# The last K and Q of batch 1: turned by DMA instead of on TensorE, with the first loads in a new order

## The chip, the cores and the metric

The kernel runs on one NeuronCore of one Trainium2 chip. The metric is the device time of one execution in microseconds (us), given as the median over runs. The engines of the core are TensorE (PE, matrix multiplication; PEld is its weight load, which overlaps), VectorE (DVE), ScalarE (ACT), GpSimd (POOL) and SyncE (SP). Here POOL does little but issue loads from HBM that cast from float32 to bf16, and SP does little but issue DMA transposes.

## The reference

Two layers, one after the other. The first is attention with a window of 32 tokens to both sides, for 8 batches of 8 heads with 576 tokens and a head size of 64. The second is a pair of dense layers (512 to 2048 to 512) with a squared ReLU between them, over all 4608 tokens.

```python
scores = scale * np.matmul(q, k.transpose(0, 1, 3, 2))
mask = np.abs(pos[:, None] - pos[None, :]) <= window
scores = np.where(mask, scores, -1000000000.0)
attn = np.exp(scores - np.max(scores, axis=-1, keepdims=True))
attn = attn / (np.sum(attn, axis=-1, keepdims=True) + 1e-09)
attn_out = np.matmul(attn, v)
x = attn_out.transpose(0, 2, 1, 3).reshape(B * S, H * D)
h = np.maximum(x @ w_in, 0.0)
out = (h * h) @ w_out
```

## The kernel before

Work is cut into 24 groups of 192 query tokens, three to a batch; group G is part g of batch b, G = 3b + g. A group has two windows, A and B, of 128 keys each. For a group the kernel does the following, and each step is an operation with a name in the program:

- It loads K, Q and V. V goes to its tile directly (`load_v`, line 443, in two pieces j = 0 and 1). The left 64 rows of V's first piece are copied from the group before (`copy_v`, line 450, on DVE).
- It turns K and Q, so that the head dimension lies on the partitions. This is done in one of two ways, below.
- It computes scores (`scores`, line 565) for all 8 heads, exponentials on ACT (line 589), the mask on DVE (line 594), and the products with V (`pv`, line 622, once for each window).
- It divides on DVE (lines 641 and 644) and turns the result into `xt`: on TensorE for the first three groups (lines 671 to 701), by two DMA transposes on SP for the others (lines 717 and 720).

The dense layers follow the tokens as they come. The up-projection (`mm1`, line 737) takes 192, later 256, later 512 tokens at a time against two slices of 128 of the 2048 hidden columns (or one slice with 512 tokens). For 192 tokens that is eight matmuls to an operation and eight operations to a block; ACT applies the ReLU (line 743), DVE squares (line 746). There are two PSUM tiles, `ht`, so an up-projection waits for the ReLU of the one before the last. The down-projection (`mm2`, line 757) takes 128 tokens and a quarter of the hidden columns at a time, four matmuls to an operation.

**K and Q, first way (groups 0 to 5).** `load_pair` loads two neighbouring tokens with one descriptor (512 bytes read, 256 written) in one DMA; a DVE copy (line 429) parts the two tokens; `turn_pe` turns the tile with eight TensorE transposes (line 485) into PSUM; ACT moves Q (line 513) and DVE moves K (line 516) to the tiles `qt` and `kt`. Group 0 alone is loaded through SP in float32 and cast on ACT and DVE (`load_hw`, lines 407 to 417).

**K and Q, second way (groups 6 to 23).** `load_qk` loads single tokens (256 bytes read, 128 written) in two DMAs, one for the first half of the tokens and one for the second; `turn_dma` turns each half with a DMA transpose that SP issues (line 524), straight into `qt` and `kt`.

**The order.** The program isn't written in the order in which it runs. Each operation is recorded with its engine, its inputs and outputs, an estimate of its duration and a key. `Prog.schedule` then plays them through: each engine takes the ready operation with the lowest key, three DMA rings (POOL, SP, ACT) share one transfer resource, and the result is a fixed order for each engine, in which `emit` writes the instructions with their semaphore waits. On the chip an engine works through its list in that order and waits where an input is late. A DMA's `slack` (`LSLACK1`, `TSLACK` and others) is a reserve added to its planned landing, so that what needs it is planned later; nothing of it is waited for on the chip.

The keys of the first loads come from the list `OPENING`, in its order: K and Q by group, V by group and piece, `w1` and `w2` the four pieces of each weight matrix, `hq` and `hk` the loads through SP. POOL issues its loads in this order, about 0.8 us apart. Loads of batch 2 and later wait for the scores of a group three before them (`gate`).

TensorE's queue is filled, while there is nothing to do at the start, with matmuls on zeros (line 322) up to the transposes of group 0's result.

`NSPLIT` says for how many groups the scores of windows A and B are recorded as two operations (eight matmuls each) instead of one (sixteen). `MKEY` and `VSET` are keys of DVE's setup of two masks and of two V tiles.

Of the kernel before, what the change touches and what calls it, by code (L numbers as in the profile page):

```python
# [20 lines left out]
NTURN = 2  # L21
NXT = 3
LEAD = 13.0
# [6 lines left out]
TDKEY = 3.0  # L30
XKEY = (0.2, 0.5)
QMOVE = 14.5
# [10 lines left out]
LSLACK = 3000  # L43
# [3 lines left out]
VCS = 6  # L47
NDUP = 1
NPR = 3
LSLACK1 = 1000  # L50
HOLD = {}
KMIN = 0.5
HOLDT = 26000
KSPL = 0
XTD = 1
NSPLIT = 3
HWB = 150
HWQ = {'k': 'SP', 'q': 'SP'}
HWC = {"k": ("DVE", "ACT"), "q": ("ACT", "DVE")}
NPAIR = 6  # L60
FIRST = {}
T512 = 2048
NBIAS = 1
PKEY = 0.2
MKEY = (-9.5, -6.5)
VSET = (-9.8, -6.8)
ESPLIT = 0
IOTA = -1
OPENING = [("k", 1), ("w1", 0), ("v", 0, 0), ("v", 1, 1), ("q", 1), ("v", 0, 1), ("q", 2), ("k", 2), ("v", 1, 0), ("w1", 1),
           ("w1", 2), ("w1", 3), ("q", 5), ("v", 2, 0), ("v", 2, 1), ("w2", 1), ("k", 3), ("v", 3, 0), ("q", 3), ("w2", 0), ("w2",  # L70
           2), ("k", 4), ("v", 3, 1), ("q", 4), ("v", 5, 0), ("v", 5, 1), ("w2", 3), ("hq", 0), ("k", 5), ("v", 4, 0), ("v", 4, 1),
           ("hk", 0)]
WARM = 40000
LAST = ((0, 256), (256, 384), (384, 512))
KC = ((0, 224), (224, 192), (416, 160))
# [204 lines left out]
class Gen:  # L280
# [105 lines left out]
    def load_qk(self, t, b, g, key):  # L386
        t0, n = KC[g] if t == "k" else (192 * g, 192)
        h = n // 2
        G = 3 * b + g
        raw = self.RAW[t][G % NRAW]  # L390
        src = (self.q if t == "q" else self.k)[b]
        s = src[:, t0:t0 + n, :].rearrange("h (j p) d -> p j h d", j=2)
        for j in range(2):
            self.p.rec("POOL", lambda e, j=j: e.dma_start(raw[0:h, j, :].rearrange("p (h d) -> p h d", h=8), s[:, j]),  # L394
                       writes=[("raw", t, G % NRAW, j)], dma=(f"{t}{G % NRAW}{j}", G), key=key, dur=500 + 3 * h,
                       move=(h // 2, QMOVE), name=f"{t}{b}{g}{j}", after=self.gate(3 * b + g), slack=LSLACK if b > 1 else 0)

    def load_hw(self, t, g, key):

# [72 lines left out]
    def turn_pe(self, t, b, g, key):  # L472
        dst, n = self.turned(t, b, g)
        h, G = n // 2, 3 * b + g
        raw = self.RAW[t][G % NRAW]
        if b:
            bank, tag = (self.AT[:, 512:1024], self.half(1)) if t == "q" else (self.AT[:, 0:512], self.half(0))
        else:
            bank, tag = (self.OUTP[0][:], ["outp0"]) if t == "k" else (self.HT[1][:], ["ht1"])
        ps = bank.bitcast(BF16)  # L480

        def f(e):
            for j in range(4):
                for x in range(2):
                    mm = e.transpose(ps[:, n * j + h * x:n * j + h * x + h], raw[0:h, x, 128 * j:128 * j + 128],  # L485
                                     self.ID[0:h, 0:h])
            return mm

        self.p.rec("PE", f, reads=[("raw", t, G % NRAW, 0), ("raw", t, G % NRAW, 1), "id"], writes=tag, key=key,
                   dur=8 * 52, name=f"turn{t}{b}{g}")  # L490
        if G < NPAIR:
            src = ps[:, 0:4 * n].rearrange("p (j r q) -> p j r q", j=4, r=2)
            dq = dst.rearrange("p j (q r) -> p j q r", r=2)
            dst = dst.rearrange("p j (q r) -> p j r q", r=2)
            if G < ESPLIT:
                self.p.rec("DVE", lambda e: e.tensor_copy(dst[:, 0:2], src[:, 0:2]), reads=tag, writes=[(t + "h", b % 2, g)],
                           key=key, dur=dve(2 * n, False), name=f"ev{t}{b}{g}h")
                self.p.rec("ACT", lambda e: e.activation(dst[:, 2:4], src[:, 2:4], ACTF.Copy), reads=tag,
                           writes=[(t + "t", b % 2, g)], key=key, dur=act(2 * n), name=f"ev{t}{b}{g}t")
                return  # L500
            dn = dve(4 * n, False)
        else:
            src = ps[:, 0:4 * n].rearrange("p (j q) -> p j q", j=4)
            dn = dve(4 * n)
        w = (t + "t", b % 2, g)
        if t == "k" and G == 0 and KSPL:
            for x, (c0, c1) in enumerate(((0, KSPL), (KSPL, h))):
                self.p.rec("DVE", lambda e, c0=c0, c1=c1: e.tensor_copy(dq[:, :, c0:c1, :].rearrange("p j q r -> p j r q"),
                                                                        src[:, :, :, c0:c1]), reads=tag,
                           writes=[("kt0", x)] if x == 0 else [w], key=key, dur=dve(8 * (c1 - c0), False), name=f"ev{t}{b}{g}{x}")  # L510
            return
        if t == "q":
            self.p.rec("ACT", lambda e: e.activation(dst, src, ACTF.Copy), reads=tag, writes=[w], key=key,
                       dur=act(4 * n), name=f"ev{t}{b}{g}")
        else:
            self.p.rec("DVE", lambda e: e.tensor_copy(dst, src), reads=tag, writes=[w], key=key, dur=dn,
                       name=f"ev{t}{b}{g}")
# [16 lines left out]
    def scores(self, G, ws):  # L534
        b, g = divmod(G, 3)
        i = b % 2
        kt, qt = self.KT[i], self.QT[i]
        key = 3 * G - LEAD + 0.3 * ws[0]
# [30 lines left out]
        rd = [("qt", i, g)] + [("kt", i, x) for x in range(max(g - 1, 0), g + 1)]  # L569
        if G == 0 and KSPL:  # L570
            rd = [("qt", i, g), ("kt0", 0)] + [("kt", i, 0)] * (1 in ws)
        two = lambda x: b >= NTURN or 3 * b + x < ESPLIT
        rd += [("qh", i, g)] * two(g) + [("kh", i, x) for x in range(max(g - 1, 0), g + 1) if two(x)]
        rd += [("ktpad", i, 0)] if g == 0 and 0 in ws else []
        rd += [("ktpad", i, 1)] if g == 2 and 1 in ws else []
# [223 lines left out]
    def build(self):  # L799
# [20 lines left out]
        for n, it in enumerate(self.opening()):  # L820
            kd, a = it[0], it[1:]
            key = K + n
            if kd == "w1":
                self.load_w1(a[0], key)
            elif kd == "w2":
                self.load_w2(a[0], key)
            elif kd == "v":
                self.load_v(*divmod(a[0], 3), key, a[1:])
            elif kd[0] == "h":
                self.load_hw(kd[1], a[0], key)  # L830
            else:
                self.load_pair(kd, *divmod(a[0], 3), key)
        for g in (1, 2, 4, 5):
            self.copy_v(g, K + 7 if g < 3 else 3 * g - LEAD - AHEAD)
        todo = []
# [1 line left out]
        def at(key, f, *a):  # L837
            todo.append((key, len(todo), f, a))

        for G in range(NG):  # L840
            b, g = divmod(G, 3)
            if b > 1:
                key = 3 * G - LEAD - (GK if G >= GFAR else AHEAD)
                for t in "kq":
                    at(key, self.load_pair if G < NPAIR else self.load_qk, t, b, g, key)
                at(key, self.load_v, b, g, key)
                if g and G < NVR:
                    key = 3 * G - LEAD - 0.5 if G >= VCS else key
                    at(key + 0.01, self.copy_v, G, key - VKEY if G >= VCS else key)
            for t in "kq":  # L850
                key = 3 * G - LEAD - (0.6 if b < NTURN else TDKEY)
                at(key, self.turn_pe if b < NTURN else self.turn_dma, t, b, g, key)
            for ws in ((0,), (1,)) if G < NSPLIT else ((0, 1),):
                at(3 * G - LEAD + 0.3 * ws[0], self.scores, G, ws)
            for w in range(2):
# [57 lines left out]
```

## Time and profile before

| | |
|---|---|
| median of 3 runs | 302.2 us (301.95 to 302.28) |
| the profiled execution, its own time | 301.87 us |
| span of its instructions | 299.9 us |
| granted TensorE clock, mean over the span | 1.000 |
| ACT busy | 160.3 us |
| DVE busy | 167.2 us |
| POOL busy | 107.1 us |
| HBM read, written | 36.70 MB, 9.44 MB |

The profile is of one execution; starts are counted from its first instruction, and the time of the execution is 2.0 us more than the span. In a timeline each row has a start and a duration in us, the engine and line, the operation with its output and input tiles, and how many instructions of the kind were merged; in brackets stands how long the engine was idle before and what ended it. An engine with a q (SPq, POOLq) is the sequencer that issues a DMA. The end of a matmul is modelled and lies some 0.2 us behind the start of the next, so the time that an operation takes of TensorE is read from one start to the next. A view by line gives for DMAs the time from the issue to the landing, that is, to the last semaphore update.

### The profile page before, as it was taken

The numbers are of one execution on the slowest core, as the hardware profiler recorded it, in microseconds if no ns is written. First come the engines' busy times: TensorE is split into PE (matmuls) and PEld (weight loads), VectorE is DVE, ScalarE is ACT, GpSimd is POOL, SyncE is SP. The second block draws the span as 40 slices with busy tenths as digits, with TensorE's granted clock in tenths as the row PEclk, the third lists the DMA queues.
The fourth block names the chain that finished last, engine by engine and source line by source line (L and its number), as shares of the span: only waits on it lengthen the run. The fifth ranks groups of instructions, "written<-read, shape, count | busy, mean of one in ns | idle before, by whom it ended". The sixth has DMA issues, their size and how long they took to land.

```text
span 299.9 us, 6209 instructions
## 1 busy us (share of the span) xinstructions
PE 291.9 (97%) x2394; PEld 171.8 (57%) x2431; DVE 167.2 (56%) x385; ACT 160.3 (53%) x250; POOL 107.1 (36%) x143
## 2 busy tenths in 40 slices
PE   7899999999999999999999999999999999999996
PEld 3578866848677767664544454444544444444445
DVE  6898775737674767563656666665666632222100
ACT  3497834836467656750765476536744643443312
POOL 8993336503544354455256335533500000000000
PEclk9999999999999999999999999999999999999999
DMA  9999999997999999999999999999992120100112
GB/s 169 176 206 184 196 177 174 169 176 137 164 169 165 95 162 146 155 138 186 180 168 131 114 166 156 125 149 156 154 128 70 55 61 35 37 35 35 38 70 105
DMA packets 160636, 39.83 MB, mean 133 GB/s; under 512 B 149984, under 2 KB 156128, under 8 KB 160608
## 3 DMA queue, kind: packets, MB, share of 16 engines
q0 software_dynamic: 106016, 17.93, 89.3%
q1 hardware_dynamic: 49264, 12.14, 28.5%
q10 hardware_dynamic: 5328, 9.37, 9.1%
q8 instruction: 19, 0.31, 0.5%
q14 instruction: 9, 0.07, 0.1%
HBM read 36.70 MB, written 9.44 MB: 154 GB/s over the span
## 4 chain that ended last, share of the span: by engine, by line
PE 90%; DMA 5%; POOL 3%; issue 1%; ACT 0%; POOLq 0%; ACTq 0%
PE ht L737 41%; PE outp L757 40%; DMA w<-in_moe_w_in_dram 5%; PE at L622 4%; PE at L565 4%; POOL v L443 1%; POOL w L456 1%; PE at L485 1%; PE ht L782 1%; PE outp L782 1%; POOL kpair L426 1%; POOL qpair L426 1%; ACT rt L743 0%; ACT oe L792 0%; POOL dif L325 0%
## 5 line engine op out<-in xcount | busy, mean ns | idle before, releaser
L737 PE MATMUL ht<-xt,w 128*128 128x256 bf16 (+2 forms) x885 | 140.0, 302 | 1.3 <-DMA w<-in_moe_w_in_dram 0.5
L757 PE MATMUL outp<-w,gt 128*128 128x512 bf16 x536 | 133.0, 379 | 1.3
L743 ACT ACTIVATE rt<-ht 128x512 bf16<-128x512 f32 (+1 forms) x152 | 85.9, 578 | 87.1 <-PE ht L737 85.1
L737 PEld LDWEIGHTS ht<-xt,w 128*128 128x128 bf16 x896 | 81.3, 98 | 43.8 <-ACT rt L743 0.6
L746 DVE TENSOR_TENSOR gt<-rt 128x512 bf16<-128x512 bf16 (+1 forms) x152 | 61.5, 408 | 61.6 <-ACT rt L743 60.0
L757 PEld LDWEIGHTS outp<-w,gt 128*128 128x128 bf16 x560 | 51.9, 98 | 54.1 <-ACT oe L767 1.0
L394 POOL DMA_DIRECT2D kraw<-in_k_dram x36 | 27.7, 778 | 107.3 <-PE at L622 56.8
L589 ACT ACTIVATE e<-at 128x1024 bf16<-128x1024 f32 x46 | 44.8, 1021 | 8.7 <-PE at L565 8.4
L594 DVE TENSOR_TENSOR pt<-e,mask 128x1024 bf16<-128x1024 bf16 x46 | 31.8, 691 | 29.0 <-ACT e L589 28.9
L443 POOL DMA_DIRECT2D v<-in_v_dram x48 | 38.2, 809 | 0.0
L767 ACT ACTIVATE oe<-outp 128x512 f32<-128x512 f32 x35 | 21.1, 604 | 29.6 <-PE outp L757 29.6
L394 POOL DMA_DIRECT2D qraw<-in_q_dram x36 | 27.7, 778 | 0.0
L622 PEld LDWEIGHTS at<-v,pt 128*128 128x128 bf16 x384 | 18.3, 98 | 9.9 <-DMA v<-in_v_dram 0.6
L622 PE MATMUL at<-v,pt 128*128 128x65 bf16 x384 | 20.1, 194 | 0.5 <-ACT pt L586 0.5
L644 DVE TENSOR_TENSOR xa<-at,rs 64x512 bf16<-64x512 f32 x24 | 16.7, 695 | 0.9
L644 DVE TENSOR_TENSOR xb<-at,rs 128x512 bf16<-128x512 f32 x24 | 16.5, 689 | 0.7
L565 PEld LDWEIGHTS at<-qt,kt 64*128 64x128 bf16 x384 | 10.8, 94 | 8.7 <-issue 7.1
L565 PE MATMUL at<-qt,kt 64*128 64x128 bf16 x384 | 15.2, 217 | 0.2
L641 DVE RECIPROCAL rs<-at 64x8 f32<-64x8 f32 (+1 forms) x48 | 10.0, 209 | 9.1 <-PE at L622 7.7
L650 DVE MEMSET at<- 64x520 f32 x23 | 11.3, 492 | 3.5 <-DVE xa L644 2.6
L450 DVE COPY v<-v 64x512 bf16<-64x512 bf16 x16 | 5.9, 372 | 5.1 <-PE ht L737 2.9
L789 DVE COPY oe<-ht 128x128 f32<-128x128 f32 x1 | 0.3, 292 | 14.5 <-PE ht L782 14.5
(67 smaller groups left out, 83.2 us busy)
## 6 DMA issues: line engine op xcount, KB each, us to landing
out_dram<-oe ACTq DMA_DIRECT2D x35, 256.0 KB, 3.2
qraw<-in_q_dram POOLq DMA_DIRECT2D x36, 96.0 KB, 5.8
w<-in_moe_w_in_dram POOLq DMA_DIRECT2D x4, 512.0 KB, 10.7
v<-in_v_dram POOLq DMA_DIRECT2D x16, 128.0 KB, 6.6
w<-in_moe_w_out_dram POOLq DMA_DIRECT2D x4, 512.0 KB, 18.8
v<-in_v_dram POOLq DMA_DIRECT2D x16, 96.0 KB, 7.0
kraw<-in_k_dram POOLq DMA_DIRECT2D x12, 112.0 KB, 4.6
kraw<-in_k_dram POOLq DMA_DIRECT2D x12, 96.0 KB, 4.9
```

The source lines that it names most:

```text
L394: self.p.rec("POOL", lambda e, j=j: e.dma_start(raw[0:h, j, :].rearrange("p (h d) -> p h d", h=8), s[:, j]), writes=[("raw", t, G % NRAW, ...
L443: self.p.rec("POOL", lambda e, j=j, lo=lo, hi=hi, k0=k0: e.dma_start(vt[lo - k0:hi - k0, j, :, 0:64], self.v[b, :, lo:hi, :].rearrange("h ...
L565: mm = e.matmul(sc[:, 512 * par + 128 * j:512 * par + 128 * j + 128], kt[r:r + 64, j, k0:k0 + 128], q, start=G >= NBIAS, stop=True, skip_g ...
L589: self.p.rec("ACT", lambda e, e_=e_, sc=sc: e.activation(e_[:], sc, ACTF.Exp, scale=0.125), reads=tags[w], writes=[("e", n % 2)], key=key, ...
L594: self.p.rec("DVE", lambda e, pt=pt, ee=ee, mb=mb: e.tensor_tensor(pt[:], ee, mb, ALU.mult), reads=[("e", n % 2), ("mask", mi)], writes=[( ...
L622: mm = e.matmul(avp[:, c:c + 65], pt[:, 4 * (h % 2) + h // 2, :], vt[:, w, h, 0:65], start=(w == 0 and y == 0), stop=True, skip_group_chec ...
L644: self.p.rec("DVE", lambda e: e.tensor_tensor(x[r0:128, :].rearrange("p (x y c) -> p x y c", x=2, y=4), av[:, :, :, 0:64], rb, ALU.mult), ...
L737: mm = e.matmul(ht[:, n * x:n * x + n], self.W1[:, ft, 128 * d:128 * d + 128], self.XT[:, ft, r:r + n], start=(ft == 0), stop=(ft == 3))
L743: self.p.rec("ACT", lambda e: e.activation(rt[:, 0:c], ht[:, 0:c], ACTF.Relu), reads=[f"ht{k % 2}"], writes=[("rt", k % 4)], key=key, dur= ...
L746: self.p.rec("DVE", lambda e: e.tensor_tensor(gt[:, d0:d0 + len(ds), r:r + n], rr, rr, ALU.mult), reads=[("rt", k % 4)], writes=[("gt", s, ...
L757: mm = e.matmul(op[:], gt[:, d, r:r + 128], self.W2[:, d, :], start=(d == 0), stop=(d == 15))
L767: self.p.rec("ACT", lambda e: e.activation(oe, op[:], ACTF.Copy), reads=[f"outp{u % 2}"], writes=[("oe", u % 4)], key=key, dur=act(512), n ...
```

## The change

Groups below `NTG` = 5 keep the first way; group 5, which was loaded as pairs and turned on TensorE, is loaded by `load_qk` and turned by `turn_dma`. In the opening list the entries of group 5 therefore stand for two DMAs each. The scores of group 5 wait for both halves. The reserve on batch 1's loads is 500 instead of 1000, and holds for `load_qk` too. The scores of group 3 are recorded as two operations. Two masks and two V tiles are set up earlier on DVE. The opening list has a new order: before the last three pieces of `w1` stand the same nine loads of POOL as before, in another order among themselves; behind them the weights `w2` and batch 1 change places.

```diff
-LSLACK1 = 1000
+LSLACK1 = 500
-NSPLIT = 3
+NSPLIT = 4
-NPAIR = 6
+NTG = 5
-MKEY = (-9.5, -6.5)
-VSET = (-9.8, -6.8)
+MKEY = (-12, -9)
+VSET = (-12, -9)
-OPENING = [("k", 1), ("w1", 0), ("v", 0, 0), ("v", 1, 1), ("q", 1), ("v", 0, 1), ("q", 2), ("k", 2), ("v", 1, 0), ("w1", 1),
-           ("w1", 2), ("w1", 3), ("q", 5), ("v", 2, 0), ("v", 2, 1), ("w2", 1), ("k", 3), ("v", 3, 0), ("q", 3), ("w2", 0), ("w2",
-           2), ("k", 4), ("v", 3, 1), ("q", 4), ("v", 5, 0), ("v", 5, 1), ("w2", 3), ("hq", 0), ("k", 5), ("v", 4, 0), ("v", 4, 1),
-           ("hk", 0)]
+OPENING = [("k", 2), ("k", 1), ("q", 2), ("v", 0, 1), ("v", 0, 0), ("q", 1), ("w1", 0), ("v", 1, 0), ("v", 1, 1), ("hq", 0),
+           ("hk", 0), ("w1", 1), ("w1", 2), ("w1", 3), ("q", 3), ("v", 2, 1), ("v", 2, 0), ("w2", 3), ("w2", 0), ("k", 3), ("q",
+           5), ("w2", 1), ("v", 3, 1), ("v", 4, 0), ("v", 3, 0), ("w2", 2), ("k", 5), ("q", 4), ("k", 4), ("v", 5, 0), ("v", 5, 1),
+           ("v", 4, 1)]
...
-                       move=(h // 2, QMOVE), name=f"{t}{b}{g}{j}", after=self.gate(3 * b + g), slack=LSLACK if b > 1 else 0)
+                       move=(h // 2, QMOVE), name=f"{t}{b}{g}{j}", after=self.gate(3 * b + g), slack=LSLACK if b > 1 else LSLACK1)
...
-        if G < NPAIR:
+        if G < NTG:
             src = ps[:, 0:4 * n].rearrange("p (j r q) -> p j r q", j=4, r=2)
...
-        two = lambda x: b >= NTURN or 3 * b + x < ESPLIT
+        two = lambda x: 3 * b + x >= NTG or 3 * b + x < ESPLIT
...
-                self.load_pair(kd, *divmod(a[0], 3), key)
+                (self.load_pair if a[0] < NTG else self.load_qk)(kd, *divmod(a[0], 3), key)
...
-                    at(key, self.load_pair if G < NPAIR else self.load_qk, t, b, g, key)
+                    at(key, self.load_pair if G < NTG else self.load_qk, t, b, g, key)
...
-                key = 3 * G - LEAD - (0.6 if b < NTURN else TDKEY)
-                at(key, self.turn_pe if b < NTURN else self.turn_dma, t, b, g, key)
+                key = 3 * G - LEAD - (0.6 if G < NTG else TDKEY)
+                at(key, self.turn_pe if G < NTG else self.turn_dma, t, b, g, key)
```

In the program that results, TensorE's order between the last piece of `w1` and the turn of group 4 differs from before. Before it runs: two up-projections, P2A (the products with V of group 2, window A), four up-projections, P2B, two, the turn of group 2's first result, one, of the second, the turn of group 3's K, one, of its Q, two, the scores of group 3, and so on. After it runs: four up-projections, P2A, the turn of group 3's Q, three, P2B, two, the turn of group 2's first result, one, of the second, two down-projections, the turn of group 3's K, two up-projections, the scores of group 3 window A, two, a down-projection, the scores of window B, one up-projection, P3A, one, a down-projection, two, P3B, three down-projections, then the turn of group 4's Q and of its K. On SP, the two transposes of group 5's Q come first, then the first half of group 3's result, the first half of group 5's K, the second half of group 3's result, the second half of K, and then batch 2.

## The prediction

> **What bounds the kernel now.** I read the page's busy times first, then the windows, then what TensorE waited for, then the timeline.
>
> ```profile
> span 299.9 us, 6209 instructions
> PE 291.9 (97%) x2394; PEld 171.8 (57%) x2431; DVE 167.2 (56%) x385; ACT 160.3 (53%) x250; POOL 107.1 (36%) x143
> ...
> 24.00:35.00 11.00, 10.89 (x158) 10.25 (x159) 8.67 (x23) 8.08 (x16) 0.94 (x3) 1.00 1.50 196
> 35.00:46.00 11.00, 10.90 (x117) 7.64 (x118) 7.87 (x19) 6.26 (x11) 4.76 (x6) 1.00 1.95 175
> 46.00:60.00 14.00, 13.89 (x150) 10.10 (x151) 9.78 (x21) 8.73 (x14) 8.96 (x12) 1.00 2.37 173
> ```
>
> TensorE (first column after the length of the window) is busy 99% from 24 us on, at a full clock. Behind that point only TensorE's work, and new holes in it, change the end.
>
> ```profile
> PE ht L737 <- DMA w<-in_moe_w_in_dram: 0.5, 1, 0.5
> PE ht L737 <- ACT rt L743: 0.2, 1, 0.2
> PE ht L737 <- issue: 0.2, 1, 0.2
> ...
> 23.25 0.40 PE L701 MATMUL at<-ident,xb 128*128 128x128 bf16 x4
> 24.11 1.48 PE L737 MATMUL ht<-xt,w 128*128 128x192 bf16 x16 [0.47 <-DMA w<-in_moe_w_in_dram]
> 25.43 0.42 PE L622 MATMUL at<-v,pt 128*128 128x65 bf16 x8
> 25.69 2.90 PE L737 MATMUL ht<-xt,w 128*128 128x192 bf16 x32
> ```
>
> These are all of TensorE's waits after 24 us, and the first is the important one: at 24.11 it waits for the last piece of the up-projection's weights. That piece was issued at 10.19 and landed 13.79 us later (the chain of waits has it), at 23.98. So the opening is bound by that transfer.
>
> **The opening, part by part.** Ahead of that piece POOL issues the same nine loads as before and the two pieces before it, and SP the same two loads; only the order among them changes. Before, they land one behind another without a hole (15.70, 18.21, 21.31, 23.98 for the last four), so the sum of bytes sets 23.98 and the order doesn't. All TensorE work planned ahead of the wait is the same work in both programs. Up-projections can start earlier because the score chain comes sooner; the gain ends in the same wait, at 24.1. I take 0. The earlier DVE setups lie in the same shadow; it has 0.5 us of cover before, and without it each us late would cost one.
>
> **TensorE work removed.** Sixteen transposes of group 5:
>
> ```profile
> 51.27 1.48 PE L737 MATMUL ht<-xt,w 128*128 128x192 bf16 x16
> 52.59 0.45 PE L485 MATMUL at<-ident,kraw 80*128 80x80 bf16 x8
> 52.87 0.51 PE L485 MATMUL at<-ident,qraw 96*128 96x96 bf16 x8
> 53.22 1.49 PE L737 MATMUL ht<-xt,w 128*128 128x192 bf16 x16
> ```
>
> Start to start, 52.59 to 53.22: **-0.63 us**. Two DVE copies (0.42 each, line 429), a move of 0.88 on DVE and one of 1.03 on ACT go as well; both engines are off the path there (9.78 and 8.73 busy of 14), so 0. The scores of group 3 split into two eights: one sixteen takes 0.55 (34.02 to 34.57), an eight 0.32 (17.14 to 17.46): **+0.09**.
>
> **New holes between 24 and 36 us.** An up-projection of eight takes 0.66 (sixteen, 24.11 to 25.43, 1.32). Its ReLU starts 0.86 after it (25.69 to 26.55) and takes 0.49; with the semaphore the same `ht` is free again 1.41 after the start, and two operations take 1.32. So two up-projections with nothing between leave 0.1. Now I walk the new order from 24.11:
>
> - The third up-projection had P2A ahead of it before; now it comes at 25.43 and its tile is free at 25.58: 0.15.
> - The turn of group 3's Q comes at 27.16; ACT moves it from 27.70 (0.54 behind, as 42.85 to 43.39) for 1.03, and the next ReLU waits behind it on ACT until 28.65, ending at 29.14. The up-projection that needs that tile could start at 28.82: 0.38.
> - K of group 3 is turned at 34.27, moved by DVE to 36.04 (as 31.20 to 32.97), and two up-projections cover only until 35.99: 0.11.
>
> Together 0.64. In the old order, 24.11 to 34.57 is 10.46, and its work, twelve up-projections (7.92), P2A and P2B (0.52), two result turns (0.44), the turns of K and Q (0.40, 0.34) and the scores (0.55), is 10.17: 0.29 of holes. Difference **+0.35**; bounds 0 (the planner's order turns out as full) and +0.6 (each hole 0.1 longer).
>
> **Loads of batch 1 on time?** This is the unknown. Walking on, TensorE reaches the turn of group 4's K at 45.9. Before, that K was in with room to spare: its load was issued at 17.90 and landed after 20.13, at 38.03, and its turn began at 42.51. Now K of group 4 stands behind all four of group 5's loads and all of W2. From the landings of before (issue plus time to landing) the spacings are: a W2 piece 2.55, a pair load of 96 rows 0.94, of 112 rows 1.25, V of 128, 96 and 64 tokens 1.05, 0.76 and 0.47. A token load has V's form (128 bytes written), so 0.76 for 96 rows, 0.63 for 80: group 5's Q 1.52, K 1.27. From 23.98: Q3 0.94, V2 1.23, two W2 pieces 5.1, K3 1.25, Q5 1.52, W2 2.55, V3 and V4 2.28, W2 2.55, K5 1.27, Q4 0.94, K4 0.94: 20.57, landing at 44.55 if nothing else moves. But two transposes of Q5 run beside them.
>
> ```profile
> 38.73 1.26 SPq L717 DMA_TRANSPOSE xt<-xa  x1
> 42.16 1.20 SPq L720 DMA_TRANSPOSE xt<-xb  x1
> 45.31 0.42 DVE L429 COPY kraw<-kpair 80x1024 bf16<-80x1024 bf16 x1 [1.25 <-DMA kpair<-in_k_dram]
> ```
>
> Before, with two transposes of 64 and 128 tokens in flight, K5's pair load of 80 rows landed 1.62 behind the load ahead of it (43.67 to 45.29), where its size asks for 0.78: 0.84 lost. Q5's two are 192 tokens again, and a part of T3a and K5 falls in too. Bounds 0 to 1.5; I take 1.0: landing at 45.55, copied by DVE (0.42 and a semaphore) at 46.1. TensorE waits **+0.2 to +0.3**; bounds 0 (landing by 45.4) and 1.0 (46.3). Behind it in TensorE's order stand two down-projections and the scores of group 4, which need nothing else: what is lost there stays lost. The other loads (V3, the third W2 piece, Q4) have about 0.2 us of room each; their lateness isn't added, since a wait shifts all that follows.
>
> The Trainium skill, "DMA: Bandwidth & Descriptors", section "Issuing engines are not separate DMA queues", speaks against this change: transfers started by any engine run on the same 16 DMA engines and interleave. By it the transposes' whole share comes on top of the loads, as in the 0.84; without it the K would land at 44.55 and nothing would wait.
>
> **SP and what it feeds.** Four more issues of 1.2 to 1.3 us stand on SP before batch 2, around the two of group 3's result. SP is idle there before (one issue at 38.73, one at 42.16, none until 47.01), so 0. The last half of K5 is issued at about 46.3 and lands by 54 (7.1 as the transposes at 47 took); the scores of group 5 come at about 55. Batch 2's loads wait for the scores of group 3, now some 2 us later; before, the scores of group 6 at 65.35 had their last transpose at 62.11, 3.2 us of cover. 0, and one for one beyond.
>
> **Sum.** -0.63 + 0.09 + 0.35 + 0.25 = +0.06 on the span of 299.9 and the time of 301.87. The profiled run stands 0.3 below the median of 302.2; the sum goes on the median: **302.3 us**, no change (within 0.2%, 0.6 us, about what a measurement of this kernel can tell from no change). With the bounds: -0.54 to +1.06, so 301.7 to 303.3.
>
> **Rivals.**
> - **Slower: K of group 4 late.** One place, TensorE's wait at the turn at 46 us, paid one for one from a landing of 45.4. If token loads cost what the first ones of batch 2 took with transposes beside them (landings at 47.99, 49.13 and 49.79, so Q 1.80; K5 in proportion 1.5), 0.5 more, and the transposes 1.5, it lands at 46.55, the turn starts at 47.1: 1.2 of wait, sum +1.0, 303.2. For: transposes took 7 us to land there, the queue is full. Against: Q5's transposes have from 34 to 45 to spread. From a landing of 46.0 on it is slower by over 0.2%. Chance 0.27. The skill's rule above leans to this one.
> - **Faster: no new holes.** ReLU holes as before and K4 at 45.4 or sooner: -0.54 and up to 0.3 if V's and K's chains overlap better: 301.4. For: the planner kept reserves. Against: the ACT move in front of the ReLU is in its order. Chance 0.18.
> - **The opening does what its order suggests**: up-projections 0.9 us earlier, kept; 301.4. It needs the last W1 piece by 23.1, with the same bytes ahead of it. Within the 0.18, a third of it.
> - **The transposes of K5 late for group 5's scores**: needs over 9 us to land; 0.03, within the slower.
>
> Forecast 0.55. Range 301.4 to 303.2, wide enough for most of both sides; the forecast's own is 301.7 to 302.8.
>
> **What would show it.** The last W1 piece still lands at 23.8 to 24.2 with TensorE's wait for it grown to about 0.9. An up-projection near 29 waits 0.3 to 0.4 for ACT, none before it that long. A wait of 0 to 0.5 of line 485 for the copy of group 4's K at 46. Line 485 has 80 matmuls instead of 96. I am wrong if that wait is over 0.8, if scores wait for transposes, or if TensorE passes 24.1 earlier.

## The result and the profile after

| | before | after |
|---|---|---|
| median of five runs, taken together | 301.95 us | 303.57 us |
| lowest and highest of after | | 302.94 and 304.32 us |
| ratio of the times, 95% interval | 1 | 1.0048 [1.0037, 1.0059] |
| the profiled execution: time, span | 301.87, 299.9 us | 303.4, 301.4 us |

The change makes the kernel 1.6 us slower. The forecast was no change, 302.3 us, with a range up to 303.2; it was wrong, and the range missed the time too. The span grew by 1.5 us, and that is what has to be found. The opening lines of after's page, and the same windows as before (columns as there; the last three are the granted clock, the share of the DMA engines and GB/s):

```profile
span 301.4 us, 6175 instructions
PE 291.9 (97%) x2376; PEld 170.0 (56%) x2412; DVE 164.5 (55%) x382; ACT 159.4 (53%) x249; POOL 108.2 (36%) x145
...
24.00:35.00 11.00, 10.66 (x131) 9.14 (x133) 6.61 (x19) 7.04 (x13) 2.06 (x3) 1.00 1.54 193
35.00:46.00 11.00, 10.76 (x113) 7.67 (x113) 7.92 (x18) 5.56 (x10) 4.81 (x6) 1.00 2.06 163
46.00:60.00 14.00, 13.69 (x147) 9.02 (x148) 8.32 (x18) 8.84 (x13) 7.41 (x10) 1.00 1.85 184
60.00:72.00 12.00, 11.50 (x102) 7.30 (x103) 5.72 (x14) 5.46 (x9) 1.66 (x3) 1.00 1.73 155
```

TensorE is less busy in each window: 10.66 where it was 10.89, 10.76 for 10.90, 13.69 for 13.89. The last window is new here; now it holds 11.50 of 12, and in before it held 11.89:

```profile
60.00:72.00 12.00, 11.89 (x102) 7.16 (x103) 6.21 (x15) 5.18 (x8) 0.09 (x1) 1.00 1.29 164
```

So the time isn't lost at one place. (The sum of busy time, 291.9 us, is that of before with 0.63 us of work removed; the ends of matmuls are modelled, so I go by windows and starts.) The lines of after's timeline (start, length, engine, line, operation) at the places that matter:

```profile
24.14 2.91 PE L737 MATMUL ht<-xt,w 128*128 128x192 bf16 x32 [0.43 <-DMA w<-in_moe_w_in_dram]
...
39.06 0.84 PE L737 MATMUL ht<-xt,w 128*128 128x192 bf16 x8
40.03 0.41 PE L622 MATMUL at<-v,pt 128*128 128x65 bf16 x8
...
46.04 0.51 PE L485 MATMUL at<-ident,qraw 96*128 96x96 bf16 x8
46.65 0.51 PE L485 MATMUL at<-ident,kraw 96*128 96x96 bf16 x8
...
67.26 1.04 PE L757 MATMUL outp<-w,gt 128*128 128x512 bf16 x4 [0.40 <-DVE gt L746]
```

The first line says that the opening gave nothing: TensorE passes the last piece of the up-projection's weights at 24.14, before at 24.11. At 39.06 eight matmuls of an up-projection start, worth 0.66 start to start; the next line starts 0.97 later, since its V piece landed at 39.90. Between the turns of group 4's Q and K lie 0.61 where Q's turn takes 0.34: K's load landed at 46.14, and TensorE waited 0.26. And at 67.26 a down-projection waits 0.40 for VectorE. That last wait is the most telling, and VectorE's timeline in after shows why:

```profile
63.03 0.69 DVE L644 TENSOR_TENSOR xb<-at,rs 128x512 bf16<-128x512 f32 x1
66.53 0.29 DVE L450 COPY v<-v 64x512 bf16<-64x512 bf16 x1 [2.81 <-DMA v<-in_v_dram]
66.84 0.36 DVE L746 TENSOR_TENSOR gt<-rt 128x384 bf16<-128x384 bf16 x1
```

VectorE stands 2.81 us at a copy of group 7's V rows (batch 2) into the tile of group 8, far from any product that needs it. The square of the ReLU (line 746), which TensorE needs next, stands behind the copy in VectorE's order. In before the same copy waited 0.95:

```profile
61.26 0.29 DVE L450 COPY v<-v 64x512 bf16<-64x512 bf16 x1 [0.95 <-DMA v<-in_v_dram]
```

The V piece was issued at 53.57 and landed at 66.50; in before it was issued at 49.77 and landed at 61.24. Of the 5.3 us, 3.8 are a later issue, since the loads of group 7 wait for the scores of group 4, which come at 48.82 instead of 45.01, and 1.5 are a longer way to landing. (The scores are the gate for batch 2; from batch 3 on it is the products with V of window B.)

So transfers land late, and in-order engines carry the lateness to TensorE. The span is 1.5 us longer with 0.63 us of work taken out and 0.1 put in, so the new holes add up to some 2 us. The named ones are 0.31 at 29 us (a ReLU behind the move of Q), 0.31 and 0.06 at the two products with V of group 3, 0.26 at 46.65 and 0.36 at 67.3. The rest are pieces of 0.1 to 0.2, some of them within what missing matmul records can fake. The DMA queues on after's page:

```profile
q0 software_dynamic: 107456, 17.93, 84.6%
q1 hardware_dynamic: 50800, 12.50, 30.1%
```

Packets, MB and share. Queue q1 carries the transposes: 49,264 packets and 12.14 MB before. The change adds 1,536 packets and 0.36 MB there, and 1,440 packets with no further bytes on q0, from loads by token (half the row length each).

### The profile page after: what moved, and what is told of

It reads as the page before. It is cut to its first block, busy times and chain, and to the rows that moved or that the text cites. A ratio compares the mean times of both kernels' runs of the same rounds, so it can differ in the third digit from the quotient of the medians.

```text
span 301.4 us, 6175 instructions
## 1 busy us (share of the span) xinstructions
PE 291.9 (97%) x2376; PEld 170.0 (56%) x2412; DVE 164.5 (55%) x382; ACT 159.4 (53%) x249; POOL 108.2 (36%) x145
## 4 chain that ended last, share of the span: by engine, by line
PE 77%; DMA 12%; POOL 8%; ACT 1%; issue 1%; DVE 1%; POOLq 0%; ACTq 0%
PE ht L737 35%; PE outp L757 35%; DMA kpair<-in_k_dram 8%; DMA v<-in_v_dram 4%; PE at L622 3%; PE at L565 3%; POOL v L443 3%; POOL w L456 1%; POOL qpair L426 1%; POOL w L461 1%; POOL kpair L426 1%; POOL qraw L394 1%; ACT e L589 1%; PE ht L782 1%; PE outp L782 1%
## 5 line engine op out<-in xcount | busy, mean ns | idle before, releaser
L394 POOL DMA_DIRECT2D kraw<-in_k_dram x38 | 29.4, 784 | 106.6 <-PE at L622 49.0
L394 POOL DMA_DIRECT2D qraw<-in_q_dram x38 | 29.3, 784 | 0.0
```

## The experiments

The theory after the first look: the four added DMA transposes and the loads by token make the loads beside them late. The rivals: the places at which the lateness happens to be caught (repair them and the change is free), and the new opening, keys and reserve.

### Repairing the places where the lateness is caught

These three kernels take the finished order of the changed kernel and move single operations in it. Nothing else moves.

```diff
+# (what, where): an operation that is put right ahead of another one in the finished order
+MOVES = [('vc8', 'M6A')]                                             # f_vc
+MOVES = [('v100', 'w21'), ('q11', 'k120'), ('k11', 'k120')]          # f_ld
+MOVES = [('vc8', 'M6A'), ('v100', 'w21'), ('q11', 'k120'), ('k11', 'k120'), ('evq10', 'r192.12')]   # f_all
...
```

`vc8` is the copy that held VectorE at 66 us, `v100` the V piece of group 3, `w21` the third W2 piece, `q11` and `k11` Q and K of group 4, `k120` the first half of group 5's K, `evq10` the move of group 3's Q on ACT.

> The changed kernel with its finished order kept, but for one step: on DVE the copy of V's left rows for group 8 (line 450) goes behind the square of the last up-projection of tokens 576 to 767 (line 746) instead of ahead of it. Theory (late loads, paid through DVE's queue): in the changed kernel that copy holds DVE 2.81 us for a V load that lands at 66.5, and TensorE waits 0.36 us for the square behind it; here the down-projection near 67 waits 0, the time falls by 0.3 to 0.5 us against the changed kernel (303.57 to about 303.2, ratio to before 1.004). Rival (the new order of TensorE's work costs the time, late loads only fill holes): another wait takes its place within 5 us and the time stays at 303.4 to 303.7.

Measured: 303.1 us (302.12 to 304.05), ratio 1.0035 [1.0023, 1.0048], against 1.0048 [1.0037, 1.0059] for the change. The hole at 67 us is gone, but in the profiled run another load was late, by more:

```profile
38.66 0.83 PE L737 MATMUL ht<-xt,w 128*128 128x192 bf16 x8
41.53 0.41 PE L622 MATMUL at<-v,pt 128*128 128x65 bf16 x8 [2.04 <-DMA v<-in_v_dram]
```

This is the product with V of group 3 that waited 0.31 in the profiled run of after. The operations and the order ahead of it are those of after, so a landing varies from run to run: this piece landed at 41.39 here and at 39.90 there. This was the slowest of the eight runs of this kernel (304.05 us); the wait isn't as long in each. The five runs of after spread over 1.4 us, the five of before beside them over 0.4.

> The changed kernel with its finished order kept, but POOL issues V piece 0 of group 3 ahead of the third W2 piece, and Q and K of group 4 ahead of group 5's K. Theory (late loads): TensorE's hole of 0.31 us ahead of the products with V of group 3 and the 0.26 us ahead of the turn of group 4's K go (K of group 4 lands near 45 instead of 46.14). But the V load that holds DVE at 66.5 doesn't land earlier, so TensorE, earlier by 0.6, waits there up to 0.9 instead of 0.36: the time gains only 0 to 0.3 us. Rival (each hole is paid for by itself): the time falls by 0.6 us, to 303.0.

Measured: 305.43 us, ratio 1.0111 [1.0097, 1.0124]. A miss, in the wrong direction. The V piece and group 4's K came in time (K landed at 45.75, not near 45). TensorE waited 0.62 for the last W2 piece instead, at 43.82. The loads of group 5's K came later for the new order, and the timelines of TensorE and then of SP in this kernel show what that did:

```profile
56.21 0.82 PE L737 MATMUL ht<-xt,w 128*128 128x192 bf16 x8 [2.21 <-DMA xt<-xb]
```

```profile
46.24 1.18 SPq L524 DMA_TRANSPOSE kt<-kraw  x1
47.46 1.68 SPq L720 DMA_TRANSPOSE xt<-xb  x1
```

SP issues in order. The transpose of group 5's K waited for its load until 46.24, and the transpose of group 3's attention result (line 720) stood behind it, 2.7 us later than in after (44.75). The tokens it turns are read at 56.21, and TensorE waited 2.21 us.

> Both of the other two edits together, and on ACT the move of group 3's Q (line 513) goes behind four more ReLUs. Theory: holes of 0.31 (V of group 3), 0.26 (K of group 4), 0.36 (square behind the V copy) and 0.3 (ReLU behind the move of Q) go, 1.2 us together: 302.2 to 302.5, no slower than 1.002 of before. Rival (new order): 303.0 or more, with new holes of the same sum elsewhere between 24 and 70 us.

Measured: 305.91 us (304.97 to 307.17), ratio 1.0129 [1.0105, 1.0153], with the same wait. A miss again. Moving the Q move behind four more ReLUs halved the hole at 29 us, 0.31 to 0.15, as meant, and was not to be seen in the time. A last repair takes the head of SP's queue away as well:

```diff
+MOVES = [('vc8', 'M6A'), ('v100', 'w21'), ('q11', 'k120'), ('k11', 'k120'), ('evq10', 'r192.12'), ('tdk12', 'tdk12')]
```

where the last entry, the first transpose of group 5's K, goes behind the second half of the result's transpose.

> The finished order of the changed kernel with six moves: the copy of V of group 8 behind the square on VectorE, the first V piece of group 3 ahead of the third W2 piece, Q and K of group 4 ahead of K of group 5 among the loads, the move of Q of group 3 behind four more ReLUs, and, new here, K's first transpose of group 5 behind the second half of the token transpose that it held up on SP. Theory (the time over before is lateness of loads that reaches TensorE through in-order queues): the wait of 2.2 us for the turned tokens at 56 us goes, a wait of some 0.6 us for the third W2 piece stays, and the time is 302.3 to 303.3. Rival (the transposes take the loads' time wherever they stand, and the lateness only finds another queue): 303.3 or more, with a new wait of over 0.6 us between 40 and 70 us.

Measured: 303.08 us, ratio 1.0037 [1.0024, 1.0049]. The time lies in the theory's interval. The trace looks like the rival, since the waits found other queues (the one for a W2 piece that was expected to stay didn't come); but the profiled run is the slowest of the five (303.91 us), and the run doesn't settle between the two. TensorE and VectorE of this kernel:

```profile
43.48 0.43 PE L622 MATMUL at<-v,pt 128*128 128x65 bf16 x8 [0.60 <-DVE at L650]
...
59.86 0.41 PE L622 MATMUL at<-v,pt 128*128 128x65 bf16 x8 [0.64 <-ACT rt L743]
```

```profile
58.74 0.29 DVE L450 COPY v<-v 64x512 bf16<-64x512 bf16 x1 [1.45 <-DMA v<-in_v_dram]
59.06 1.29 DVE L594 TENSOR_TENSOR pt<-e,mask 128x1024 bf16<-128x1024 bf16 x2
```

The first hole is 0.76 against its neighbour's starts and the second 0.80; neither was there in after. At the second the wait is put down to ACT, whose ReLU had nothing to do with it: what came late is the masked softmax (line 594), which stood on VectorE behind yet another copy of V. VectorE waited 7.9 us for V in four copies between 24 and 80 us, 1.8 in before. By the ratios, four repairs together bring no more than the one copy alone (1.0037 and 1.0035, for 1.0048 of the change).

### Which part of the change costs

> The changed kernel with that one part undone: group 5 by pairs and turned on TensorE again; opening, keys, reserve and split of the changed kernel are kept, and the order is planned anew. Theory: the loads are no later than in before (second V piece of group 7 of batch 2 landed near 61 us), and the time is that of before or up to 0.6 us more, 302.0 to 302.7, for the fourth split and a re-planned order. Rival (opening, keys and reserve cost): 303 to 304, as the changed kernel.

```diff
 # the changed kernel
-NTG = 5
+NTG = 6
```

Measured: 302.29 us, ratio 1.0007 [0.9998, 1.0015]. The new opening, the keys, the reserve of 500 and the split of group 3's scores cost nothing that can be told. The 0.30 hole behind the Q move at 29 us is still there.

> The kernel before with only one part of the change: K and Q of group 5 loaded by token and turned by four DMA transposes; opening, keys and reserve are those of before. The order is planned anew, so other operations move too; the plan itself leaves TensorE a hole of 0.96 us near 32 us. Theory (the four transposes and the loads by token make the loads beside them late, whatever the opening is): 303 to 305 us, landings of the V pieces of batch 2 later than in before by 3 us or more, waits for V, W2 or K on TensorE between 40 and 70 us. Rival (the new opening, keys and reserve are what costs): within 0.3 us of before, 301.8 to 302.4, with 0.6 us of it gone from TensorE at the turns.

```diff
 # the kernel before
-NPAIR = 6
+NTG = 5
...
-        if G < NPAIR:
+        if G < NTG:
...
-                key = 3 * G - LEAD - (0.6 if b < NTURN else TDKEY)
-                at(key, self.turn_pe if b < NTURN else self.turn_dma, t, b, g, key)
+                key = 3 * G - LEAD - (0.6 if G < NTG else TDKEY)
+                at(key, self.turn_pe if G < NTG else self.turn_dma, t, b, g, key)
```

Measured: 304.99 us, ratio 1.009 [1.0075, 1.0104]. Group 5 by token and by DMA alone costs more than the whole change. Not all of it is the transposes, though: the order planned anew has a hole of its own of 0.96 us in the plan, and the trace shows 0.97 at 35.4 us, where the turn of group 3's Q waits for its copy and the copy for its load. So the size can't be read from this run.

> The order of before on every engine, with K and Q of group 5 each as two loads by token (pieces of half the size, twice the packets), still turned on TensorE; no transposes. Theory that the transposes are what delays: the V pieces of batch 2 land at most 1 us later than in before and the time is 301.9 to 302.4. Rival, that the loads by token are the larger share: landings 2 us or more later and 303 us or more.

```diff
 # the kernel before, its order kept; group 5 only: two loads by token into the same tile
+    a, c = [Half(pr[0:h, 512 * j:512 * j + 512].rearrange("p (h d) -> p h d", h=8), s[j]) for j in range(2)]
...
+        ops.insert(ops.index(a) + 1, o)
```

Measured: 301.91 us, ratio 0.9999 [0.9991, 1.0007]. The loads by token, with their doubled packets, are free. The last V pieces of groups 6 and 7 landed at 53.80 and 62.48, 1.8 and 1.2 us later than in before, over the 1 us that was expected, and no wait on TensorE came of it.

### The transposes by themselves

```diff
 # the kernel before, its order kept
+    # four transposes of W1 (as wide as group 5's Q and K) into a tile that nothing reads
+        o.fn = lambda e: e.dma_start(prog.scr[:, :, 96 * x:96 * x + n], prog.w1t[0:n, 0, 0:512], transpose=True)
...
+    k = ops.index(named["T3a"])
+    ops[k:k] = [op(0, 96, "q12"), op(1, 96, "q12")]
+    k = ops.index(named["T3b"]) + 1
+    ops[k:k] = [op(2, 80, "w23"), op(3, 80, "w23")]
```

> The kernel before, its order untouched, with four more DMA transposes on SP of a weight tile into a tile that nothing reads: two of 96 tokens when Q of group 5 has landed (about 32 us), two of 80 behind the transposes of group 3's result (about 44 us), as wide as those that the change adds. Nothing waits for them. Theory (transposes slow the loads beside them by more than the 0.84 us for 192 tokens that the prediction took): the V loads of group 6 and 7 that landed at 52.03 and 61.24 land 3 us or more later, DVE waits longer for V before its copy, and the time rises by 0.2 to 1.0 us. Rival (the double packets of the token loads make them late): those landings move by less than 1.5 us and the time stays within 0.2 us of before.

Measured: 304.28 us (303.86 to 304.75), ratio 1.0073 [1.006, 1.0086]: four transposes that nothing waits for cost 2.2 us. TensorE in this kernel:

```profile
40.91 0.41 PE L622 MATMUL at<-v,pt 128*128 128x65 bf16 x8 [0.52 <-DMA v<-in_v_dram]
45.57 1.04 PE L757 MATMUL outp<-w,gt 128*128 128x512 bf16 x4 [0.48 <-DMA w<-in_moe_w_out_dram]
```

Both are waits for loads, and before had none of them. TensorE's order is that of before, so its starts can be laid beside those of before: it loses 0.68 us at the first and 0.69 at the second, and some 0.5 in smaller pieces. Is it transposing, or any 0.36 MB on SP at these places? The next run makes the four plain copies of the same bytes:

```diff
-        o.fn = lambda e: e.dma_start(prog.scr[:, :, 96 * x:96 * x + n], prog.w1t[0:n, 0, 0:512], transpose=True)
+        o.fn = lambda e: e.dma_start(prog.scr[0:n, x, :], prog.w1t[0:n, 0, 0:512])
```

> As the run with four transposes that nothing reads, but the four are plain copies of the same bytes (rows of 1 KB of W1 into a tile that nothing reads), at the same places of SP's order with the same waits. Theory that the price is the transposing, the many small packets on the DMA engines: the V pieces of batch 2 land within 1 us of before and the time is within 0.5 us of it, 302.0 to 302.6. Rival that it is SP's order, the waits or the bytes: landings 2 us or more later and 303.5 or more, as with the four transposes.

Measured: 302.66 us, ratio 1.0022 [1.0013, 1.0031]. By the time the theory holds: 0.5 us of 2.2 go with the bytes and the places, the rest with transposing. By the landings it was too simple, since V of group 7 landed 2.2 us late here too, and the last piece of group 6 2.6 (54.59 for 52.03). What separates the runs are the loads of batch 1. K of group 4 landed at 38.03 in before, at 38.18 with loads by token and at 38.52 with the four copies, but at 39.65 with the four transposes; the last W2 piece at 43.67, 44.05 and 44.23, but at 45.52. The same tile's view in this kernel and in the one with transposes (the form and its time on SP, then the time to landing, least, median and most):

```profile
L920 SPq DMA_DIRECT2D scr<-w x4: 522/587/613, 31.8 to 44.8; - x4
...
DMA to landing us min/median/max: 5.3/6.1/6.9
```

```profile
L920 SPq DMA_TRANSPOSE scr<-w x4: 1177/1268/1297, 31.7 to 46.8; - x4
...
DMA to landing us min/median/max: 6.3/7.2/7.9
```

A transpose holds SP for 1.27 us where a copy of the same bytes holds it for 0.59, and lands 1.1 us later. On the page's queue lines the four transposes add 1,536 packets and the four copies 416. The number of packets alone isn't the price, since the loads by token added 1,440 on their own queue at no cost; what in a transpose slows its neighbours stays open.

Two halves of the same kernel, the first two transposes alone (96 tokens each, at the place of Q's) and the last two alone (80 each, at K's):

> Only the first two of the four unread transposes, 96 tokens each, at the place of those of Q. If each costs the loads the same 0.9 us of landing: V pieces of batch 2 some 1.8 us later than in before; first waits on TensorE for V of group 3 and the last W2 piece of 0.2 to 0.4 us each; time 302.6 to 303.5. Rival, that two fit into the loads' reserve and only four go over it: 302.0 to 302.3.

Measured: 303.6 us, ratio 1.005 [1.0037, 1.0063], just over the expected interval. The waits came where they were expected, but the first is 1.29 us instead of 0.2 to 0.4, and it isn't a wait for V. TensorE, then VectorE:

```profile
41.49 0.43 PE L622 MATMUL at<-v,pt 128*128 128x65 bf16 x8 [1.29 <-DVE at L650]
```

```profile
40.41 0.42 DVE L429 COPY kraw<-kpair 96x1024 bf16<-96x1024 bf16 x1 [1.74 <-DMA kpair<-in_k_dram]
40.94 0.49 DVE L650 MEMSET at<- 64x520 f32 x1
```

The copy of group 4's K waits 1.74 us for its load (landed at 40.38), and the memset that clears the next product's place in PSUM stands behind it. V itself landed at 41.11, so without the copy the product would have come only some 0.2 us earlier. SP issued nothing between these two transposes (31.6 to 34.3) and 38.70, so it isn't their time on SP's queue that costs.

> Only the last two of the four unread transposes, 80 tokens each, at the place of those of K (near 46 us). They start behind the waits that the run with four showed at 41 and 45 us, so those two waits (0.68 and 0.64 us) stay away; V pieces of batch 2 some 1.7 us later; time 302.2 to 302.9. Rival, that the late stretch is what costs: 303 or more.

Measured: 303.17 us, ratio 1.004 [1.0028, 1.0052], again over the expected interval. The waits at 41 and 45 us stayed away as expected. V of group 7 landed 3.3 us late instead of 1.7 (0.5 of it issued later). VectorE, then TensorE:

```profile
64.52 0.29 DVE L450 COPY v<-v 64x512 bf16<-64x512 bf16 x1 [3.61 <-DMA v<-in_v_dram]
```

```profile
66.54 0.62 PE L565 MATMUL at<-qt,kt 64*128 64x128 bf16 x16 [0.58 <-issue]
```

The copy of V held VectorE for 3.61 us. The scores of group 6 waited 0.58 us; the profile names nothing for it, but the divide behind the copy, which frees their place in PSUM, ends at 66.43. Some 0.4 us of this profiled run were lost ahead of the added transposes (TensorE passes the last piece of `w1` at 24.53). The two halves cost 1.4 and 1.0 us; together, in the run with four, 2.2.

### The gain by itself

```diff
-            for j in range(4):
-                for x in range(2):
+            for j in range(4 if G != 5 else 1):
+                for x in range(2 if G != 5 else 1):
...
-            src = ps[:, 0:4 * n].rearrange("p (j r q) -> p j r q", j=4, r=2)
+            src = (ps if G != 5 else self.W1[:, 0])[:, 0:4 * n].rearrange("p (j r q) -> p j r q", j=4, r=2)
```

> The order of before on every engine, with 14 of the 16 TensorE transposes that turn K and Q of group 5 left out (two of 16 stay; the copies behind them read W1 in place of the turned values, so group 5's scores are not those of the reference). Leaves out only the gain side of the change: by the sum of the prediction 0.63 us for sixteen, so 0.55 us for fourteen if nothing else ends the path there: 301.4 to 301.7. Rival: that the time is hidden by another wait: 301.9 to 302.2.

Measured: 301.87 us, ratio 0.9993 [0.9984, 1.0002], 0.3 us below the 302.18 of before beside it: between the two expectations, and not told from no change. TensorE in this kernel:

```profile
53.76 0.20 PE L485 MATMUL at<-ident,kraw 80*128 80x80 bf16 x1
53.80 0.21 PE L485 MATMUL at<-ident,qraw 96*128 96x96 bf16 x1
53.84 1.49 PE L737 MATMUL ht<-xt,w 128*128 128x192 bf16 x16
55.46 0.62 PE L565 MATMUL at<-qt,kt 64*128 64x128 bf16 x16
```

From the first turn to the up-projection are 0.08 us where there were 0.63, so the 0.55 is there. But the scores come 1.62 after that up-projection's start and not 1.41: they now wait for the move of Q on ACT, which starts after the turn as before and ends at 55.40. In the changed kernel that move is gone, so this loss of 0.2 belongs to the experiment. The profiled run is the slowest of the twelve (302.75 us); it shows where the starts lie, not the time.

Side by side, without the other repairs and the replanned order, with the second V piece of group 7 in the profiled run (it is issued later where TensorE has lost time ahead of it); the time is the difference to the median of before in the same set of runs:

| kernel | added transposes | V of group 7 issued, us | landed, us | time, us |
|---|---|---|---|---|
| before | 0 | 49.77 | 61.24 | 0 |
| group 5 by pairs again, all else of the change | 0 | 51.98 | 60.55 | +0.2 |
| loads by token alone | 0 | 50.08 | 62.48 | -0.2 |
| four plain copies | 0 | 50.00 | 63.44 | +0.5 |
| first two transposes | 2 | 51.66 | 61.43 | +1.4 |
| last two transposes | 2 | 50.31 | 64.50 | +1.0 |
| four transposes | 4 | 51.30 | 64.90 | +2.2 |
| the change | 4 | 53.57 | 66.50 | +1.6 |
| the change, four repairs | 4 | 53.59 | 67.76 | +1.0 |

The four transposes (+2.2), the gain (-0.3 to -0.6) and the loads by token (0) sum to +1.6 to +1.9, and the change measured +1.6. The parts were measured in the order of before and the change has an order of its own, so that they add up is an agreement and no proof. The landing of this one piece doesn't rank the times: it is later with four copies (+0.5) than with the first two transposes (+1.4), whose cost was paid earlier, at the loads of batch 1. Every kernel with an added transpose is slower than before by about 1 us or more, and no kernel is faster than before by more than can be told. At both places that were tried, a pair of transposes costs more than the half of 0.63 us that it saves.

## Why the prediction was wrong, point by point

- **The opening, 0.** Right. Landing at 24.09 for 23.98, TensorE past it at 24.14 for 24.11. The sign that was named for it, a wait for that piece grown to about 0.9, didn't show: 0.43 for 0.47, so TensorE came to that wait no earlier.
- **TensorE work removed, -0.63.** Right in size: 0.55 of fourteen sixteenths went from TensorE where the transposes were left out; the time of that kernel fell by 0.3, which isn't told from none.
- **Scores of group 3 split, +0.09.** Right: two times 0.326 for 0.553, so 0.10.
- **New holes, +0.35.** Right in sum, +0.31: 0.09 at the third up-projection (forecast 0.15), 0.31 behind the move of Q (0.38), none more than usual before the scores (0.11), less the 0.09 that before has at 27.09. That it costs was not shown: with the split and the largest hole kept and the transposes undone the time is that of before.
- **K of group 4 late, +0.25.** Right in the wait, 0.26. The landing was put at 45.55 and was 46.14: 1.6 us of lateness on the sum of 44.55, where 1.0 was taken and 1.5 was the bound; TensorE came later as well. The main rival on the slower side, at 303.2 us, named this place alone and asked 1.2 us of it. It gave a time near the true one for a wait that wasn't there.
- **The step that failed** lies in the part on batch 1's loads, in what it says of the others: they "have about 0.2 us of room each; their lateness isn't added, since a wait shifts all that follows", together with the 0 for batch 2's loads under their "3.2 us of cover". (The 0 for SP held: the last half of group 5's K landed at 53.83, and by 54 was forecast.) Three things in it were wrong. First, the price of the transposes was worked out for one load, K of group 4, and charged there only; the runs show that it goes to a whole row of loads. Two transposes issued at 31.6 and 33.0 us, of 192 tokens together, made the nine loads of batch 1 and W2 that landed after 38 us come 1.3 to 2.4 us late (two W2 pieces at 34.17 and 36.99 came as before): K of group 4 first (40.38 for 38.03), then the last W2 piece (45.89 for 43.67) and at the end the last V piece of batch 1 (48.17 for 46.57), against the 0.84 per 192 tokens that was used. In the change itself, V of group 3 landed at 39.90 where the prediction's own sum puts it at 38.85, and TensorE waited 0.31 for it. The last V pieces of groups 6 and 7 came late too, but by 1.2 to 2.6 us in the runs with loads by token and with copies as well, so the transposes' share in them isn't separated. Second, the cover of batch 2 was read from one consumer, the scores of group 6. The consumer that stands still first is the copy of V on VectorE, ahead of squares, masks and divides that TensorE needs; it already waited 0.95 us in before, so the load had no cover there. What the copy's wait costs TensorE depends on what stands behind it: 2.81 us cost 0.40 in after and 3.61 cost 0.58 in the run with the last two transposes, while 3.02 in the run with four gave no wait that the profile names. The loads of group 7 were also issued 3.8 us later, where the prediction counted some 2 for the loads of batch 2. Third, a wait that shifts all that follows doesn't pay for the next one: with the four unread transposes TensorE lost 0.68 us for V of group 3 and then 0.69 more for W2. Landings scatter besides, so that different loads are the late one in different runs.
- **The signs of being wrong** that the prediction named (a wait over 0.8 for group 4's K, scores that wait for group 5's transposes, TensorE past 24.1 earlier) all stayed away. The loss came at places that none of them watched.
- **The rule that was weighed**, from the Trainium skill's "DMA: Bandwidth & Descriptors", section "Issuing engines are not separate DMA queues", says that transfers of all issuing engines run on the same 16 engines and interleave. The run with four transposes agrees: issued by SP, read by nobody, 2.2 us. It was used as a reason for one term, where it bore on the whole stretch.
- The Trainium skill's "VectorE: DVE Perf Modes", section "Rules for kernel authors", advises TensorE for a turn of 128 by 128 if PSUM will do as its target, and the DMA otherwise. The runs here agree: 0.63 us on a TensorE that is busy 99% of the stretch for sixteen turns of 80 and 96 tokens is cheaper than the 2.2 us of four unread DMA transposes of the same width.

## What to carry to other kernels

Moving work from a full TensorE to DMA isn't free if loads are in flight: price an added transfer by all the loads in flight beside it (here loads that landed up to 16 us after the first transposes were issued came late), and test it alone, as a transfer that nothing reads, before anything else is rebuilt around it. The cover of a load is the slack of its first consumer and of everything behind that consumer on an in-order engine, not the slack of the matmul that needs the data. When repairs of single waits move the wait rather than shorten the time, look for what the late transfers share, and test that by itself.

## What the runs showed of the hardware

- A DMA transpose costs its neighbours far more than its bytes: four of them (0.36 MB) cost 2.2 us, four plain copies of the same bytes 0.5 us. The Trainium skill's "Advanced Engine Details and Errata", section "X-Bar Transpose (TRN2)", calls transposes as fast as regular transfers; here a transpose of 80 or 96 tokens held SP 1.27 us against 0.59 and took a median of 7.2 us to land against 6.1, so in this kernel the measurement differs.
- Halving the row length of one group's K and Q loads, and so doubling their packets (1,440 more), cost nothing: 0.9999 [0.9991, 1.0007].
- A single load can land 1.5 us later in one run than in another at the same place of the order: V of group 3 landed at 39.90 in the profiled run of after and at 41.39 in that of the kernel that differs from it only by a copy 25 us later. TensorE waited 0.31 for it in the one and 2.04 in the other.
